# Chunk and weight loads issued further ahead, x laid out by chunks, two weight tiles converted among the first chunks

## The chip, the cores and the metric

The kernel runs on one core of one Trainium2 chip. The metric is the device time of one execution in microseconds. Three runs of the kernel before gave 604.84, 605.93 and 606.35 us; their median is 605.93 us.

## The reference

Three stages in a row, all in float32. First a gated linear attention with a state of 48 x 48 per head (batch 4, heads 8, 768 tokens, head size 48):

```python
f = 1.0 / (1.0 + np.exp(-f_logit))
for t in range(S):
    state = f[:, :, t, :, None] * state + np.einsum('bhd,bhe->bhde', k[:, :, t], v[:, :, t])
    y[:, :, t] = np.einsum('bhd,bhde->bhe', q[:, :, t], state)
```

Its result is put together to x of 3072 tokens x 384. Second a two-layer network with 2048 hidden units and a squared ReLU:

```python
h = np.maximum(x @ w_in, 0.0)
x = h * h @ w_out
```

Third a soft mixture of eight experts with four slots each: logits `x @ phi`, a softmax over the tokens that makes 32 slot inputs, two expert layers on those 32 rows, and a softmax over the slots that spreads their results back to the tokens.

## The kernel before

**Attention by chunks.** The 3072 tokens are cut into 24 chunks of 128 (six to each batch entry). A chunk needs one load of f, k and q together (`fkq`, 672 KB) into one of three slots g0 to g2 (`slot`, `SLOTS = 3`), and one of v (192 KB, `chunk_load`, lines 129 to 139) into one of three buffers. `prep(i)` (lines 144 to 182) makes running products of the gates and scales k and q with them: exponentials and logarithms on ScalarE (L156, L158, L169, L170), scans (L162) and products (L171, L177, L178, L179) on VectorE. Its last product, L179, is the last reader of the slot. `chunk(i)` (lines 270 to 281) has TensorE's part in five steps: transposes and their copy (L193, L195), scores (L205, L208), the state (L220, L228), values (L243, L250) and the result y (L254, L259). At its end SP issues six DMAs that put y into x, transposed and by rows: two of 72 KB (L265), two of 16 KB and two of 8 KB (L268).

**The two-layer network.** Four chunks make a block of 512 tokens, so x has six blocks (b) of [128, 3, 512], the 384 features in three groups of 128 (kt). The hidden units are cut into 16 tiles of 128 (ff). A step is one pair (b, ff): `layer1` and `layer2`. To keep float32 precision, x and the weights are each split into a high and a low part (`hl`: a cast on ScalarE, L113, and a difference on VectorE, L114), and every product becomes three matmuls of 512 columns (`mm3`, lines 118 to 120): nine for layer 1 (ph) and nine for layer 2 (o). 92 of the 96 steps go this way. The first four steps, block 0 with tiles 0 to 3, use unsplit float32 weights instead (`layer1_whole` L353, L384), whose matmuls take longer but need only the converted tile.

**Weights.** A tile's input and output weights come as 64-bit floats in one load of 768 KB (`w_load`, L305, `raw<-w`). `w_split` (lines 308 to 340) converts it to float32 in integer arithmetic: L315 and L319 on ScalarE, L320 and L321 on VectorE, and a last sum that makes the tile whole (L331 for tiles 0 to 3, L333 for the others). `w_parts` splits it. `WAHEAD = 4` says how many tiles are asked for ahead of the one that is converted. Raw, whole and split tiles share 16 buffers.

**Order.** `fast` and `fast_blocks` (lines 675 to 822) write the work down in one order. First chunks 0 to 2 and tiles 0 and 1 are loaded. `stream` then walks through the chunks: chunk i's five steps, with the preparation of a later chunk between them, and the load of a later one: chunk 3 after the last step of chunk 0, chunk 4 after that of chunk 1 (tiles 2 and 3 with them), and from chunk 3 on the load of chunk i + 2 behind the second step of chunk i. `upto(n)` advances the stream to its n-th step. After 23 steps (chunk 4, third step) tile 0 is converted and the steps of the network begin; step n = 0, 1, 2 each convert one more tile, from step 4 on each step converts the tile of its number, and each asks for tiles up to WAHEAD further on. The order of the steps is block 0 with tiles 0 to 3, block 1 with tiles 0 to 8, block 0 with the rest, block 1 with the rest (`TURNS`), and then block by block; the remaining chunks are worked in between (`target`).

This written order isn't the order on the engines. A planner takes it as a priority, estimates when each operand is ready, and gives every engine a fixed sequence from that: an instruction whose operands it believes to be there is put ahead of earlier written ones that still wait. For instance chunk 3's load stands on SP ahead of chunk 0's result, which is written first. At run time each engine works through its sequence strictly in order and waits where something is late. All DMAs here are issued by SP.

**The tail.** After the last block come the expert layers (`tail`, lines 575 to 672) and the output.

Of the kernel before, what the change touches and what calls it, by code (L numbers as in the profile page):

```python
# [18 lines left out]
HR = 64  # L19
# [15 lines left out]
LEAD = 4  # L35
SLOTS = 3
RAW = 5
WAHEAD = 4
AHEAD = 5
FIRST = 23  # L40
WARM = (3, 1, 3, 3)
# [1 line left out]

TURNS = ((0, 0, 4), (1, 0, 9), (0, 4, NFF), (1, 9, NFF))
ONACT = range(2, 8)
WHOLE = TURNS[0][2]
ORDER = (1, 0) + tuple(range(2, NB))
SECOND = 46
# [9 lines left out]
class K:  # L58
# [70 lines left out]
    def chunk_load(self, i):  # L129
        nc, ap = self.nc, self.ap  # L130
        fkq = self.slot(i % SLOTS)[:DD].rearrange("d (x p t) -> d x p t", x=3, p=NP)
        if i == 0:
            nc.sync.dma_start(out=fkq[:, 0], in_=self.A["fkq"][i][:, 0])
            nc.sync.dma_start(out=fkq[:, 1:], in_=self.A["fkq"][i][:, 1:])
        else:
            nc.sync.dma_start(out=fkq, in_=self.A["fkq"][i])
        v = ap.tile([128, DM], F32, tag="v", name="v", bufs=3)
        nc.sync.dma_start(out=v, in_=self.A["v"][i])
        return fkq[:, 0], fkq[:, 1], fkq[:, 2], v

# [91 lines left out]
    def values(self, i):  # L232
# [26 lines left out]
                nc.vector.tensor_tensor(y[:, :, r], y[:, :, r], py[j], ALU.subtract)  # L259
        if c == 0:  # L260
            self.x_alloc(b)
        xl = self.x[b][1].bitcast(F32)
        ts = slice(c * C, (c + 1) * C)
        for h in range(2):
            nc.sync.dma_start(out=xl[h * D : h * D + D, :, ts], in_=y[h * HR : h * HR + D, :KT])  # L265
        for h in range(2):
            for e, n, kt, o in PLACE[6 + h]:
                nc.sync.dma_start(out=xl[o : o + n, kt, ts], in_=y[h * HR + e : h * HR + e + n, KT])  # L268

    def chunk(self, i):  # L270

# [10 lines left out]


    def x_alloc(self, b):
        x = self.x_room(b % 2).rearrange("p (x k t) -> p x k t", x=2, k=KT)
        self.x[b] = x[:, 0], x[:, 1]

    def x_room(self, j):
        return self.fp.tile([128, 2 * KT * TB], F32R, tag=f"x{j}", name="x", bufs=1)

    def x_split(self, b, kt):
        xh, xl = self.x[b]
        self.hl(xh[:, kt], xl[:, kt], xl[:, kt].bitcast(F32))

    def w_load(self, ff):

# [50 lines left out]
    def layer1_whole(self, b, ff):  # L347

        nc, fp = self.nc, self.fp
        x, w = self.x[b][1].bitcast(F32), self.whole[ff]  # L350
        o = self.ps.tile([128, 512], F32, tag="h", name="ph", bufs=2)[:, :TB]
        for kt in range(KT):
            nc.tensor.matmul(out=o, lhsT=w[:, kt * 128 : kt * 128 + 128], rhs=x[:, kt], start=kt == 0, stop=kt == KT - 1)  # L353
        r = fp.tile([128, TB], F32, tag="r", name="r", bufs=1)
        nc.scalar.activation(r, o, AF.Relu)
        g = fp.tile([128, TB], F32, tag="gl", name="g2", bufs=2)
        nc.scalar.activation(g, r, AF.Square)
        return g, None

    def layer1(self, b, ff):  # L360
        nc, fp = self.nc, self.fp
        x, w = self.x[b], self.w[ff]
        ph = self.ps.tile([128, 512], F32, tag="h", name="ph", bufs=2)
        o = ph[:, :TB]
        for kt in range(KT):
            ks = slice(kt * 128, kt * 128 + 128)
            self.mm3(o, w[:, 0, ks], w[:, 1, ks], x[0][:, kt], x[1][:, kt], kt == 0, kt == KT - 1)
        r = fp.tile([128, TB], F32, tag="r", name="r", bufs=1)
        nc.scalar.activation(r, o, AF.Relu)  # L369
        gh = fp.tile([128, TB], F32R, tag="gh", name="gh", bufs=2)  # L370
        nc.scalar.activation(gh, r, AF.Square)  # L371
        nc.scalar.activation(r, r, AF.Square)  # L372
        gl = fp.tile([128, TB], F32R, tag="gl", name="gl", bufs=2)
        nc.vector.tensor_tensor(gl, r, gh.bitcast(F32), ALU.subtract)  # L374
        return gh, gl
# [320 lines left out]
    def fast_blocks(self, main, pst, ast, wst, raw):  # L696

        def stream():
            for i in range(2):
                yield from self.prep(i)  # L700
            for i in range(NCH):
# [3 lines left out]
                for j, n in enumerate((1, 1, 0, 0, 2) if ahead == 2 else (1, 1, 1, 0, 2)):  # L705
                    next(ch)
                    for _ in range(n):
                        next(pr, None)
                    new = i + 3 if i < 2 else i + 2
                    if j == (4 if i < 2 else 1) and i != 2 and new < NCH:  # L710
                        self.loaded[new] = self.chunk_load(new)
                        if new < 5:
                            more_w()
                    yield

# [2 lines left out]
                raw[len(raw)] = self.w_load(len(raw))  # L718

        st = stream()  # L720
        for _ in range(8):
            next(st)
        done = 0
        end = NCH * STEPS

# [22 lines left out]

        def split(b):
            if b in unsplit:  # L750
                for kt in range(KT):
                    self.x_split(b, kt)
                unsplit.remove(b)

        def begin1(b, ff):
# [6 lines left out]
        def part(ff):  # L762
            if ff in self.whole and ff not in self.w:
                self.w_parts(ff, self.whole[ff])

        upto(FIRST)
        unsplit = list(ORDER)
        self.w_split(0, raw[0], True)
        wn = 1
        posts = iter(())  # L770
        pend = begin1(0, 0)
        wait = 0
        for n, (b, ff) in enumerate(steps):
            if n == 3:
                self.consts3()
            if wn < WHOLE or WHOLE <= n and wn < NFF:
                while len(raw) < min(NFF, wn + WAHEAD):
                    more_w()
                self.w_split(wn, raw[wn], wn < WHOLE)
# [59 lines left out]
    def slow(self):  # L839
# [3 lines left out]
        with ExitStack() as main:  # L843
# [13 lines left out]
            with ExitStack() as st:  # L857
                self.pp = self.pool(st, "pp2")
                for b in range(NB):
                    self.x_alloc(b)  # L860
                    xh, xl = self.x[b]
                    self.hl(xh, xl, xT[:, :, b * TB : (b + 1) * TB])
                    for ff in range(NFF):
                        self.layer2(b, ff, self.layer1(b, ff), ff == 0, ff == NFF - 1)
                    for _ in self.post(b):
# [120 lines left out]
```

## Time and profile before

| what | value |
|---|---|
| median of three runs | 605.93 us |
| the profiled execution | 606.27 us |
| its span, first to last instruction | 604.5 us |
| TensorE (PE) busy | 574.9 us, 95% |
| TensorE weight loads (PEld) busy | 442.4 us, 73% |
| VectorE (DVE) busy | 328.7 us, 54% |
| ScalarE (ACT) busy | 314.8 us, 52% |
| DMA: time of packets on the data queue, share of 16 engines | 35.8% |
| moved | 69.59 MB |

The 1.77 us between the execution and its span lie ahead of the first and behind the last instruction. The busy time of TensorE is modelled at the ends of matmuls, which overlap, so a full TensorE is seen in the step from one matmul to the next (0.23 us for 512 columns at full clock) more than in the share. The kernel falls into stages: the first chunks with a start of the network (to some 87 us), the network with the remaining chunks (to some 545 us) and the tail.

### The profile page before, as it was taken

What the parts mean: (1) busy time and instruction counts of PE and PEld (TensorE: products, weight loads), DVE (VectorE), ACT (ScalarE), POOL (GpSimd) and SP (SyncE); (2) the same over time, 40 slices, a digit from 0 to 9 for tenths busy, and PEclk for the clock granted to TensorE, in tenths of its full rate; (3) what the DMA queues carried; (4) which work ended last, traced back from release to release, by engine and by line L of the source; (5) the groups of instructions that cost most, each with busy time, mean ns of one, the idle gap of its engine ahead of it and who ended that gap; (6) DMA issues with size and microseconds to landing.
All of it is one profiled execution on the core that took longest, in us unless ns stands there. A gap on an engine that the chain in (4) does not pass through costs nothing.

```text
span 604.5 us, 13326 instructions
## 1 busy us (share of the span) xinstructions
PE 574.9 (95%) x5587; PEld 442.4 (73%) x5587; DVE 328.7 (54%) x688; ACT 314.8 (52%) x577; POOL 4.0 (1%) x10
## 2 busy tenths in 40 slices
PE   4899899999999999999999999999999999998993
PEld 3784467788787878778877777887788887886372
DVE  6978989999825547454464552543332322213322
ACT  5647759996635546354455354544334544442122
POOL 0000000000000000000000000000000100000000
PEclk9999979999999999999999999999999999999898
DMA  9557558421321202202211210220000745554757
GB/s 290 181 154 236 160 190 287 151 67 47 105 60 40 73 2 73 59 16 73 73 46 28 74 63 18 79 79 3 15 14 12 263 135 177 168 199 157 262 205 272
DMA packets 28324, 69.59 MB, mean 115 GB/s; under 512 B 4464, under 2 KB 17008, under 8 KB 28256
## 3 DMA queue, kind: packets, MB, share of 16 engines
q1 hardware_dynamic: 28256, 68.65, 35.8%
q8 instruction: 46, 0.75, 0.5%
q14 instruction: 22, 0.18, 0.1%
HBM read 59.20 MB, written 4.72 MB: 106 GB/s over the span
## 4 chain that ended last, share of the span: by engine, by line
PE 77%; DVE 7%; DMA 6%; ACT 6%; issue 2%; SPq 1%; ACTq 0%; DVEq 0%
PE o L118 10%; PE ph L118 9%; PE o L120 9%; PE ph L120 9%; PE ph L119 9%; PE o L119 9%; DMA g<-fkq 4%; PE psm L243 3%; DMA raw<-w 2%; DVE ip L162 2%; PE hp L591 2%; PE psm L220 2%; PE psm L205 2%; PE so L615 2%; PE o L384 1%
## 5 line engine op out<-in xcount | busy, mean ns | idle before, releaser
L374 DVE TENSOR_TENSOR gl<-r,gh 128x512 fp32r<-128x512 f32 x92 | 63.5, 690 | 119.2 <-ACT r L372 118.6
L369 ACT ACTIVATE r<-ph 128x512 f32<-128x512 f32 x92 | 54.7, 595 | 119.9 <-PE ph L120 114.9
L118 PE MATMUL o<-gh,w 128*128 128x512 f32 x276 | 112.8, 409 | 0.0
L118 PE MATMUL ph<-x,w 128*128 128x512 f32 x276 | 111.5, 404 | 0.0
L119 PE MATMUL o<-gh,w 128*128 128x512 f32 x276 | 108.0, 391 | 0.0
L120 PE MATMUL o<-gl,w 128*128 128x512 f32 x276 | 106.3, 395 | 1.8 <-DVE gl L374 1.7
L120 PE MATMUL ph<-x,w 128*128 128x512 f32 x276 | 107.8, 391 | 0.0
L119 PE MATMUL ph<-x,w 128*128 128x512 f32 x276 | 107.6, 390 | 0.0
L120 PEld LDWEIGHTS o<-gl,w 128*128 128x128 f32 x276 | 51.6, 188 | 15.7 <-DVE gl L374 4.8
L118 PEld LDWEIGHTS ph<-x,w 128*128 128x128 f32 x276 | 51.8, 188 | 14.7 <-issue 4.1
L118 PEld LDWEIGHTS o<-gh,w 128*128 128x128 f32 x276 | 51.7, 187 | 12.6 <-ACT gh L371 0.5
L120 PEld LDWEIGHTS ph<-x,w 128*128 128x128 f32 x276 | 51.8, 188 | 11.5
L371 ACT ACTIVATE gh<-r 128x512 fp32r<-128x512 f32 x92 | 58.3, 634 | 2.0
L119 PEld LDWEIGHTS ph<-x,w 128*128 128x128 f32 x276 | 51.9, 188 | 9.7
L372 ACT ACTIVATE r<-r 128x512 f32<-128x512 f32 x92 | 58.0, 630 | 1.8
L119 PEld LDWEIGHTS o<-gh,w 128*128 128x128 f32 x276 | 51.9, 188 | 9.4
L156 ACT ACTIVATE g<-g 112x512 f32<-112x512 f32 (+1 forms) x25 | 15.1, 609 | 41.8 <-DMA g<-fkq 41.8
L243 PEld LDWEIGHTS psm<-q,S 48*48 48x48 f32 (+1 forms) x704 | 27.2, 147 | 9.7 <-issue 4.6
L243 PE MATMUL psm<-q,S 48*48 48x64 f32 (+1 forms) x704 | 31.5, 244 | 2.5 <-DVE S L226 1.3
L162 DVE TENSOR_TENSOR_SCAN ip<-g,ip,big 112x128 f32<-112x128 f32 x80 | 33.4, 467 | 0.4 <-ACT g L158 0.2
L220 PEld LDWEIGHTS psm<-v,n 64*48 64x48 f32 (+1 forms) x704 | 21.3, 146 | 10.8 <-issue 5.3
L169 ACT ACTIVATE g<-ip 112x512 f32<-112x512 f32 (+1 forms) x25 | 15.3, 611 | 26.2 <-DVE ip L162 26.1
(143 smaller groups left out, 683.0 us busy)
## 6 DMA issues: line engine op xcount, KB each, us to landing
m<-m SPq DMA_DIRECT2D x26, 768.0 KB, 4.4
g<-fkq SPq DMA_DIRECT2D x23, 672.0 KB, 5.2
raw<-w SPq DMA_DIRECT2D x16, 768.0 KB, 7.1
v<-v SPq DMA_DIRECT2D x24, 192.0 KB, 3.6
g<-m SPq DMA_DIRECT2D x6, 768.0 KB, 4.5
out_dram<-ob SPq DMA_DIRECT2D x18, 256.0 KB, 3.3
x<-y SPq DMA_DIRECT2D x48, 72.0 KB, 2.8
x<-y SPq DMA_DIRECT2D x48, 16.0 KB, 1.8
```

Source lines behind the costliest of these rows:

```text
L118: mm(out=out, lhsT=sh, rhs=mh, start=start, stop=False)
L119: mm(out=out, lhsT=sl, rhs=mh, start=False, stop=False)
L120: mm(out=out, lhsT=sh, rhs=ml, start=False, stop=stop)
L156: nc.scalar.activation(f[:, s], f[:, s], AF.Exp, scale=-1.0)
L162: nc.vector.tensor_tensor_scan(ip[:, p], f[:, p], big, 1.0 if first else self.ip[:, p, C - 1 : C], ALU.mult, ALU.min)
L169: nc.scalar.activation(f[:, s], ip[:, s], AF.Ln)
L220: nc.tensor.matmul(out=pu[c][m, p], lhsT=U["n"][r, p, m], rhs=U["v"][r, hd * D : hd * D + D], start=True, stop=True)
L243: nc.tensor.matmul(out=pz[h * HR : h * HR + m, p, r], lhsT=U["S"][c][d, p * D : p * D + m], rhs=U["q"][d, p, r], start=True, stop=True)
L369: nc.scalar.activation(r, o, AF.Relu)
L371: nc.scalar.activation(gh, r, AF.Square)
L372: nc.scalar.activation(r, r, AF.Square)
L374: nc.vector.tensor_tensor(gl, r, gh.bitcast(F32), ALU.subtract)
```

## The change

- `WAHEAD` goes from 4 to 6, and v has four buffers instead of three.
- The load of chunk 3 and of tiles 2 and 3 is asked for right after the first eight steps of the stream, which are the preparations of chunks 0 and 1.
- The load of chunk i + 3 (not i + 2) is asked for behind the second step of chunk i, for i from 1 to 20, and one more weight tile with it if fewer than WAHEAD are loaded ahead.
- Tile 0 is converted after 8 steps of chunks (third step of chunk 1) and tile 1 after 18 (third step of chunk 3), instead of at 23 and in step 0. Tiles 2 and 3 are converted in steps 0 and 1 instead of 1 and 2.
- x is laid out as [chunk, kt, 128 tokens] instead of [kt, 512 tokens]. A chunk's larger result DMA then writes 1536 bytes in a row in each partition instead of three times 512; a matmul of layer 1 reads its 512 columns as four runs of 128; the split of x goes by chunks (four operations of 384 columns on each engine) instead of by kt (three of 512).

```diff
-WAHEAD = 4
+WAHEAD = 6
+FIRSTW = 8, 18
...
-        v = ap.tile([128, DM], F32, tag="v", name="v", bufs=3)
+        v = ap.tile([128, DM], F32, tag="v", name="v", bufs=4)
...
-        xl = self.x[b][1].bitcast(F32)
-        ts = slice(c * C, (c + 1) * C)
+        xl = self.x[b][1].bitcast(F32)[:, c]
         for h in range(2):
-            nc.sync.dma_start(out=xl[h * D : h * D + D, :, ts], in_=y[h * HR : h * HR + D, :KT])
+            nc.sync.dma_start(out=xl[h * D : h * D + D], in_=y[h * HR : h * HR + D, :KT])
...
-        x = self.x_room(b % 2).rearrange("p (x k t) -> p x k t", x=2, k=KT)
+        x = self.x_room(b % 2).rearrange("p (x c k t) -> p x c k t", x=2, c=NC, k=KT)
...
-    def x_split(self, b, kt):
+    def x_split(self, b, c):
         xh, xl = self.x[b]
-        self.hl(xh[:, kt], xl[:, kt], xl[:, kt].bitcast(F32))
+        self.hl(xh[:, c], xl[:, c], xl[:, c].bitcast(F32))
...
-            self.mm3(o, w[:, 0, ks], w[:, 1, ks], x[0][:, kt], x[1][:, kt], kt == 0, kt == KT - 1)
+            self.mm3(o, w[:, 0, ks], w[:, 1, ks], x[0][:, :, kt], x[1][:, :, kt], kt == 0, kt == KT - 1)
...
-                    new = i + 3 if i < 2 else i + 2
-                    if j == (4 if i < 2 else 1) and i != 2 and new < NCH:
-                        self.loaded[new] = self.chunk_load(new)
-                        if new < 5:
+                    if j == 1 and 0 < i < NCH - SLOTS:
+                        self.loaded[i + SLOTS] = self.chunk_load(i + SLOTS)
+                        if len(raw) < wn + WAHEAD:
                             more_w()
...
         st = stream()
+        wn = 0
         for _ in range(8):
             next(st)
+        self.loaded[SLOTS] = self.chunk_load(SLOTS)
+        for _ in range(2):
+            more_w()
...
+        for n in FIRSTW:
+            upto(n)
+            self.w_split(wn, raw[wn], True)
+            wn += 1
         upto(FIRST)
         unsplit = list(ORDER)
-        self.w_split(0, raw[0], True)
-        wn = 1
...
-            if wn < WHOLE or WHOLE <= n and wn < NFF:
+            if wn < min(WHOLE, n + 3) or WHOLE <= n and wn < NFF:
```

What is left out takes the same layout of x through `layer1_whole`, the copy out of layer 1 and a second path of the kernel that these inputs don't take.

## Rows read from the trace of the kernel before

**Rows 1.** The page's first part: busy us (share of the span) and instructions.

```profile
PE 574.9 (95%) x5587; PEld 442.4 (73%) x5587; DVE 328.7 (54%) x688; ACT 314.8 (52%) x577; POOL 4.0 (1%) x10
```

**Rows 2.** Windows by stage: PE, PEld, DVE, ACT, POOL busy, PEclk, DMA share, GB/s.

```profile
0.00:15.00 15.00, 6.12 (x117) 5.39 (x118) 9.36 (x27) 7.46 (x15) 1.10 (x8) 1.00 0.91 288
...
8.00:45.00 37.00, 32.15 (x634) 29.01 (x637) 31.12 (x70) 20.07 (x37) 0.00 (x0) 1.00 0.68 205
45.00:87.00 42.00, 38.71 (x451) 22.01 (x443) 36.41 (x72) 29.17 (x53) 0.00 (x0) 0.92 0.62 182
87.00:150.00 63.00, 62.82 (x485) 49.53 (x484) 62.32 (x104) 54.02 (x96) 0.00 (x0) 1.00 0.45 151
150.00:190.00 40.00, 38.42 (x282) 30.10 (x280) 21.18 (x45) 21.91 (x40) 0.00 (x0) 1.00 0.27 71
190.00:545.00 355.00, 354.36 (x3136) 282.01 (x3137) 155.28 (x332) 172.31 (x318) 2.85 (x2) 1.00 0.25 75
```

**Rows 3.** The chain of waits, 20 to 100 us: start, us, what.

```profile
30.69 7.15 DMA raw<-w
...
64.78 7.78 DMA raw<-w
```

**Rows 4.** Timeline of ScalarE: start, us, instruction, [idle before <- what ended it].

```profile
18.56 0.91 ACT L315 ACTIVATE raw<-raw 128x768 int32<-128x768 uint32 x1
...
27.65 0.91 ACT L315 ACTIVATE raw<-raw 128x768 int32<-128x768 uint32 x1 [1.42 <-DMA raw<-w]
29.90 0.63 ACT L156 ACTIVATE g<-g 112x512 f32<-112x512 f32 x1 [1.33 <-DMA g<-fkq]
...
37.86 0.93 ACT L315 ACTIVATE raw<-raw 128x768 int32<-128x768 uint32 x1 [2.35 <-DMA raw<-w]
...
42.68 0.63 ACT L156 ACTIVATE g<-g 112x512 f32<-112x512 f32 x1 [1.78 <-DMA g<-fkq]
...
72.59 0.97 ACT L315 ACTIVATE raw<-raw 128x768 int32<-128x768 uint32 x1 [1.40 <-DMA raw<-w]
```

**Rows 5.** Waits of TensorE, 0 to 87 us: total us, times, longest.

```profile
PE psm L220 <- ACT n L195: 2.1, 1, 2.1
...
PE ph L353 <- DVE wn L331: 0.9, 1, 0.9
```

**Rows 6.** Windows of 3 us around the late stall, columns as in rows 2.

```profile
72.00:75.00 3.00, 0.93 (x36) 0.65 (x33) 3.00 (x7) 2.41 (x5) 0.00 (x0) 1.00 0.30 57
75.00:78.00 3.00, 2.96 (x24) 1.37 (x26) 1.97 (x5) 1.75 (x3) 0.00 (x0) 0.58 1.04 302
78.00:81.00 3.00, 3.00 (x80) 2.94 (x77) 2.14 (x4) 0.66 (x2) 0.00 (x0) 0.50 0.68 257
81.00:84.00 3.00, 3.00 (x9) 1.44 (x7) 2.51 (x5) 2.35 (x5) 0.00 (x0) 0.78 0.13 29
```

**Rows 7.** Timeline of SP's DMA issues, 0 to 60 us.

```profile
8.90 0.33 SPq L136 DMA_DIRECT2D g<-fkq  x1
...
22.64 0.53 SPq L138 DMA_DIRECT2D v<-v  x1
...
36.57 0.58 SPq L136 DMA_DIRECT2D g<-fkq  x1
```

**Rows 8.** The differences of line 114 by shape: ns min/median/max, first and last start.

```profile
L114 DVE TENSOR_TENSOR x<-x x18: 682/685/693, 74.2 to 471.6; 128x512 fp32r<-128x512 f32 x18
L114 DVE TENSOR_TENSOR w<-whi,w x12: 930/950/959, 81.8 to 144.5; 128x768 fp32r<-128x768 f32 x12
```

**Rows 9.** Timelines of SP and VectorE around a late chunk load.

```profile
155.36 20.23 SPq L136 DMA_DIRECT2D g<-fkq  x2
...
174.51 0.69 DVE L179 TENSOR_TENSOR q<-g,t 112x512 f32<-112x512 f32 x1 [2.52 <-PE psm L243]
```

**Rows 10.** The chain of waits: a wide matmul and a group of short ones.

```profile
161.36 0.23 PE o L118
...
249.07 1.01 PE psm L243 x29
```

More of the change, by code (lines that the diff above doesn't have):

```diff
@@ L261, in values @@
             self.x_alloc(b)
-        xl = self.x[b][1].bitcast(F32)
-        ts = slice(c * C, (c + 1) * C)
+        xl = self.x[b][1].bitcast(F32)[:, c]
         for h in range(2):
-            nc.sync.dma_start(out=xl[h * D : h * D + D, :, ts], in_=y[h * HR : h * HR + D, :KT])
+            nc.sync.dma_start(out=xl[h * D : h * D + D], in_=y[h * HR : h * HR + D, :KT])
         for h in range(2):
             for e, n, kt, o in PLACE[6 + h]:
-                nc.sync.dma_start(out=xl[o : o + n, kt, ts], in_=y[h * HR + e : h * HR + e + n, KT])
+                nc.sync.dma_start(out=xl[o : o + n, kt], in_=y[h * HR + e : h * HR + e + n, KT])
     def chunk(self, i):
@@ L352, in layer1_whole @@
         for kt in range(KT):
-            nc.tensor.matmul(out=o, lhsT=w[:, kt * 128 : kt * 128 + 128], rhs=x[:, kt], start=kt == 0, stop=kt == KT - 1)
+            nc.tensor.matmul(out=o.rearrange("p (c t) -> p c t", c=NC), lhsT=w[:, kt * 128 : kt * 128 + 128], rhs=x[:, :, kt], start=kt == 0, stop=kt == KT - 1)
         r = fp.tile([128, TB], F32, tag="r", name="r", bufs=1)
@@ L363, in layer1 @@
         ph = self.ps.tile([128, 512], F32, tag="h", name="ph", bufs=2)
-        o = ph[:, :TB]
+        o = ph[:, :TB].rearrange("p (c t) -> p c t", c=NC)
         for kt in range(KT):
             ks = slice(kt * 128, kt * 128 + 128)
-            self.mm3(o, w[:, 0, ks], w[:, 1, ks], x[0][:, kt], x[1][:, kt], kt == 0, kt == KT - 1)
+            self.mm3(o, w[:, 0, ks], w[:, 1, ks], x[0][:, :, kt], x[1][:, :, kt], kt == 0, kt == KT - 1)
         r = fp.tile([128, TB], F32, tag="r", name="r", bufs=1)
-        nc.scalar.activation(r, o, AF.Relu)
+        nc.scalar.activation(r, ph[:, :TB], AF.Relu)
         gh = fp.tile([128, TB], F32R, tag="gh", name="gh", bufs=2)
@@ L750, in split @@
             if b in unsplit:
-                for kt in range(KT):
-                    self.x_split(b, kt)
+                for c in range(NC):
+                    self.x_split(b, c)
                 unsplit.remove(b)
@@ L861, in slow @@
                     xh, xl = self.x[b]
-                    self.hl(xh, xl, xT[:, :, b * TB : (b + 1) * TB])
+                    self.hl(xh, xl, xT[:, :, b * TB : (b + 1) * TB].rearrange("p k (c t) -> p c k t", c=NC))
                     for ff in range(NFF):
```

## The prediction

> **What bounds the kernel now.** First the page's busy shares: TensorE counts as busy for 95% of the span [rows 1], so the question is where it isn't, or where it runs slowly. Second the busy time by stage [rows 2]. From 87 us to 545 us TensorE is full but for 0.18 us in 87 to 150, 1.58 us in 150 to 190 and 0.64 us after; that work is the same before and after. What can move the end is the stage ahead of it: from 8 to 87 us TensorE lacks 4.85 + 3.29 us, VectorE 5.88 + 5.59 us. Third, the chain of waits between 20 and 100 us: its two longest pieces are loads of weight tiles, 7.15 us from 30.69 and 7.78 us from 64.78 [rows 3]. Such a piece is not all loss: while a load is under way the engines do other work, and only the end of it holds someone. Who is held is read from ScalarE's timeline [rows 4]: converts (L315) wait 1.42, 2.35 and 1.40 us for a weight tile, and exponentials (L156) 1.33 and 1.78 us for a chunk. ScalarE runs its queue in order, so what stands behind a waiting convert waits too. At 72.59 that is, two operations on, the copy L195, for which TensorE waits 2.1 us [rows 5].
>
> That late stall costs twice. By windows of 3 us [rows 6], TensorE is busy for 0.93 us in 72 to 75, and then the granted clock falls to 0.58, 0.50 and 0.78 of full speed in the next three: the lower of its two levels (1.2 of 2.4 GHz) for (1 - 0.58) / 0.5 x 3 = 2.5, then 3.0 and 1.3 us, together 6.8 us.
>
> **The change part by part,** against the profiled execution: 606.27 us, its span 604.5; the median of the runs is 605.93, 0.34 below.
>
> *Weight loads earlier.* Tiles 2 and 3 are issued behind the results of chunks 0 and 1 now, tile 2 right after the value load v of chunk 3 at 22.64, which waits for one of three v buffers [rows 7], tile 3 at 30.69 [rows 3]. With the fourth v buffer, and both tiles asked for right after chunk 3, they can follow that chunk's load at 8.90 [rows 7]. Tiles 4 to 7 each move from a step of the network (tile 6: 64.78 [rows 3]) to chunks 1 to 4, tile 6 by some 25 us, and SP has no more to issue than before. So the waits of L315 should go. The late one: 2.1 us of TensorE, **-2.1**. With it the fall of the clock: half of 6.8 us is 3.4 us, but VectorE works for 6.62 of the 9 us [rows 6], so no more than 2.4 comes out before it is late next: **-2.4** (ends 0, if TensorE goes idle elsewhere, and -3.4, if VectorE's work there can come earlier).
>
> *Chunk loads earlier.* Chunk 5's load is issued at 36.57 [rows 7], behind chunk 2's result; its slot, chunk 2's, is free from that chunk's preparation on, well before its result. Asked for a chunk earlier it stands behind chunk 1's result, at about 30 us, and the waits of 1.33 and 1.78 us go. Together with the early converts ScalarE waits 1.42 + 1.33 + 2.35 + 1.78 = 6.88 us [rows 4]. That can't all be gained: TensorE lacks 4.85 us in 8 to 45, VectorE 5.88, and part of both is the recurrence from chunk to chunk. Ends 0 and -4.9; I take the middle, **-2.5**.
>
> *Two tiles converted among the first chunks.* The products L331 of tiles 0 and 1 (0.95 us of VectorE each, L331 ends when the tile is whole) come some steps earlier, and tiles 2 and 3 one step earlier each. TensorE waits for such a tile once, 0.9 us [rows 5]. Price: two products more in a stretch in which VectorE has 5.88 us free. I take **-0.5** (ends +1.0 and -0.9).
>
> *x by chunks.* A split is four pairs of operations of 384 columns in place of three of 512. VectorE takes 685 ns for 512 columns and 950 for 768 [rows 8], so 555 for 384: 4 x 555 - 3 x 685 = +0.17 us a block. Four of six blocks are split where VectorE is half idle [rows 2]; blocks 0 and 1 lie in the full stretch: **+0.3**. ScalarE's part is as small and has room there. The result's larger DMA writes runs of 1536 bytes instead of 512, the four small ones stay, and SP issues as many as before: nothing, since the last small one ends the group. The matmuls read x in four runs of 128 columns: no row shows that, and I cost it at nothing (ends 0 and a rival below).
>
> *Late holes.* The 1.58 us in 150 to 190 belong to chunk loads that wait for a slot: SP stands 20.23 us in two issues from 155.36, until VectorE's L179 at 174.51 has read the slot [rows 9]. Slots stay three, so asking earlier doesn't help: nothing (ends -1.6 and +1.0, the same hole again).
>
> *Handed back.* What comes earlier than 87 us meets a stretch where VectorE has 0.68 of 63 us free. From 8 to 150 it has 12.15 us free in all, of which the 7.5 would take more than half; I charge **+1.0** (ends 0 and +4).
>
> Sum: -2.1 - 2.4 - 2.5 - 0.5 + 0.3 + 1.0 = -6.2, so 600.1 in the profiled execution and **599.7** as a median.
>
> **The rivals.**
> *ScalarE held at the start (slower).* The planner puts converts well ahead of the code's place (tile 6's convert belongs to step 6, and it runs before step 4 begins). If it puts tile 2's where tile 1's is now, at 18.56 us [rows 4], it waits for a queue that is already full: the loads issued up to 10 us would be four chunks of 672 + 192 KB, four tiles of 768 KB and 96 KB of constants, 6.8 MB, at the 288 GB/s of the first 15 us [rows 2] landed 23.5 us after 1.5, at 25 us. ScalarE would stand 6.4 us in front of the chunks, and the early gain of 2.5 would go: 599.7 + 2.5 + 6.4 = 608.6. It decides from a stand of 3.7 us on. For it: three such waits in the trace now. Against: even crowded, the tiles land before the 27.65 and 37.86 at which they are converted now [rows 4]. The Trainium skill's DMA: Bandwidth & Descriptors (Queues, rings and completion order) says that each DMA engine consumes the descriptors of one issuer's row in ring order; by that a chunk's load behind two weight tiles would wait for both. In rows that is the same stand with an exponential in the convert's place: two tiles of 768 KB at 288 GB/s are 5.5 us, and 599.7 + 2.5 + 5.5 = 607.7; its chance is part of this rival's. No row here tells ring order from mere crowding.
>
> *x's runs cost TensorE (slower).* 828 matmuls of layer 1 would restart at three breaks each. The nearest row is the short matmuls L243: 1.01 us for 29 of 64 columns, 35 ns each, against 0.23 us / 512 x 64 = 29 ns of a wide one [rows 10], so at most 6 ns a break: 828 x 3 x 6 ns = +14.9, 614.6. It turns the sign from 2.5 ns on. Against it: the wide matmul's columns lie next to each other in runs of 512 bytes. The Trainium skill's SBUF — State Buffer (Door 1, the note on cachelines) puts the penalty of a stride at crossings of 16-byte lines, of which the breaks add none; no run here shows it yet.
>
> *VectorE gives half back.* The moved products and exponentials only queue on VectorE before 150 us: half of 6.2, so 603.
>
> *Everything goes.* Late 2.1 + 3.4, early 4.9, the tile 0.9, the holes 1.6, nothing handed back: -12.9 + 0.3, so 605.93 - 12.6 = 593.3.
>
> *The loads don't really move.* The planner or a full queue leaves weights and chunks where they land now: 605.5 to 606.5.
>
> **How the numbers follow.** Forecast 0.42 (597.5 to 602), everything 0.17, half back 0.15, no change 0.10, ScalarE held 0.12, x's runs 0.04. A run of this kernel can be told from no change by about 0.3%, 1.8 us. Faster: 0.42 + 0.17 + 0.13 of half back = 0.72; same 0.02 + 0.10 = 0.12; slower 0.16. The range 594 to 608 leaves out x's runs, half of ScalarE held and the lower half of everything, about 0.18.
>
> **What would show it.** Right: tiles 2 and 3 issued near 10 us, tile 6 before 45; no wait of L315 over 1 us; granted clock 1.00 from 60 to 90; the first split matmul (L118, now where the stage from 87 us begins) some 6 us earlier, and the distance from there to the end unchanged. Wrong: L315 waiting at 16 to 25 us; a new stretch of half clock; a wide matmul's step above 0.23 us in layer 1 and not in layer 2; VectorE full before 87 with TensorE waiting for it; holes after 150 that grow by what the start gained.

## The result, and the profile after

The changed kernel takes 609.42 us (median of four runs, 609.33 to 609.94); the kernel before, on the same chip, 605.38 us (604.49 to 606.35). The ratio is 1.0068, 95% interval [1.0049, 1.0087]: slower by 0.7%, and 1.4 us above the end of the forecast range. The profiled execution has a span of 607.6 us against 604.5.

The first split matmul of the network, the milestone that the forecast named, starts at 92.67 us. Before, it started at 86.9: it is 5.8 us later, not 6 earlier. From there to the end 514.9 us pass instead of 517.6. 5.8 - 2.7 = 3.1 us is the whole difference of the spans.

In the kernel after, a line up to the result's DMAs has a number one higher than before: L157 is L156 of the kernel before. The windows by stage, columns as in [rows 2]:

```profile
8.00:45.00 37.00, 28.49 (x583) 25.85 (x585) 31.39 (x70) 21.86 (x40) 0.00 (x0) 1.00 0.95 288
45.00:87.00 42.00, 39.28 (x476) 24.11 (x472) 37.16 (x74) 28.96 (x53) 0.00 (x0) 1.00 0.55 164
87.00:150.00 63.00, 59.90 (x420) 46.69 (x419) 60.61 (x103) 49.93 (x88) 0.00 (x0) 0.97 0.37 119
150.00:190.00 40.00, 39.83 (x346) 31.99 (x346) 20.92 (x44) 22.53 (x39) 0.00 (x0) 1.00 0.23 65
190.00:545.00 355.00, 354.42 (x3137) 281.81 (x3136) 156.68 (x337) 174.51 (x324) 2.85 (x2) 1.00 0.24 73
```

Against [rows 2]: the clock of 45 to 87 us is back at 1.00, but TensorE lacks 8.51 us in 8 to 45 (4.85 before), and a new hole of 3.10 us stands in 87 to 150 (0.18 before). The holes of 150 to 190 shrank from 1.58 to 0.17.

What the forecast said of the loads came. SP's issues in the kernel after: tiles 2 and 3 together near 10 us, tile 6 at 41 us.

```profile
10.40 0.96 SPq L305 DMA_DIRECT2D raw<-w  x2
...
41.36 0.43 SPq L305 DMA_DIRECT2D raw<-w  x1
```

And ScalarE's waits from 0 to 125 us (total, times, longest) for a chunk and for a tile; before, the same two lines of this view had 6.7 us in 5 waits and 5.2 us in 3, the long ones of which are in [rows 4]:

```profile
ACT g L157 <- DMA g<-fkq: 3.9, 2, 2.4
...
ACT raw L315 <- DMA raw<-w: 0.7, 1, 0.7
```

So data came earlier, and the network's full stage began later. Where is seen in the timeline of ScalarE after (start, length, instruction, [idle before <- what ended it]):

```profile
30.97 0.60 ACT L255 ACTIVATE y<-psm 112x512 f32<-112x512 f32 x1 [2.92 <-PE psm L244]
...
33.61 0.91 ACT L319 ACTIVATE whi<-raw 128x768 f32<-128x768 f32 x1 [0.34 <-DVE wn L331]
...
34.51 0.62 ACT L157 ACTIVATE g<-g 112x512 f32<-112x512 f32 x1
...
35.70 0.91 ACT L315 ACTIVATE raw<-raw 128x768 int32<-128x768 uint32 x1
38.53 0.63 ACT L170 ACTIVATE g<-ip 112x512 f32<-112x512 f32 x1 [1.92 <-DVE ip L163]
...
39.73 0.58 ACT L255 ACTIVATE y<-psm 112x512 f32<-112x512 f32 x1
...
46.35 0.63 ACT L170 ACTIVATE g<-ip 112x512 f32<-112x512 f32 x1 [3.22 <-DVE ip L163]
...
48.18 0.59 ACT L255 ACTIVATE y<-psm 112x512 f32<-112x512 f32 x1
...
92.11 0.51 ACT L114 CAST x<-x 128x384 fp32r<-128x384 f32 x1 [2.92 <-issue]
```

and in that of VectorE:

```profile
30.49 0.56 DVE L320 TENSOR_SCALAR whi<-whi 128x768 int32<-128x768 int32 x1
31.08 0.96 DVE L321 SCALAR_TENSOR_TENSOR whi<-raw,whi 128x768 int32<-128x768 int32 x1
...
32.62 0.95 DVE L331 CUSTOM_DVE_ANT_0 wn<-raw,whi 128x1536 uint16<-128x1536 uint16 x1
...
35.01 0.55 DVE L320 TENSOR_SCALAR whi<-whi 128x768 int32<-128x768 int32 x1
...
35.97 0.95 DVE L321 SCALAR_TENSOR_TENSOR whi<-raw,whi 128x768 int32<-128x768 int32 x1
36.83 1.60 DVE L163 TENSOR_TENSOR_SCAN ip<-g,ip,big 112x128 f32<-112x128 f32 x4
```

From 30.49 to 36.92 us VectorE does 0.56 + 0.96 + 0.95 + 0.55 + 0.95 = 3.97 us of weight conversion, and only then chunk 4's scan L163. On ScalarE chunk 4's exponential (L157) stands behind L319 of these conversions and starts at 34.51; before, it started at 29.90 [rows 4]. Its logarithm L170 then waits 1.92 us for the scan, and the copy of chunk 3's result (L255, 39.73) stands behind that. In the timeline of ScalarE before, the same two pairs of logarithm and copy are

```profile
34.22 0.63 ACT L169 ACTIVATE g<-ip 112x512 f32<-112x512 f32 x1 [0.97 <-DVE ip L162]
...
38.69 0.57 ACT L254 ACTIVATE y<-psm 112x512 f32<-112x512 f32 x1
...
44.80 0.60 ACT L254 ACTIVATE y<-psm 112x512 f32<-112x512 f32 x1 [1.49 <-PE psm L243]
...
47.66 0.63 ACT L169 ACTIVATE g<-ip 112x512 f32<-112x512 f32 x1 [1.23 <-DVE ip L162]
```

Chunk 4's logarithm stood ahead of chunk 3's copy before as well, but it ran at 34.22. For the next pair the order itself has turned: chunk 5's logarithm (46.35) now stands ahead of the copy of chunk 4's result (48.18), where before it stood behind it (47.66 against 44.80). So conversions of weights that come early hold a chunk's preparation, and an instruction for a later chunk holds the result of an earlier one. That the planner put them there because it believed their data to be there follows from how it works; its estimates aren't in the trace.

On TensorE the order has changed on a larger scale. Its timeline after, at the start of the network and at the first split matmul:

```profile
56.15 6.83 PE L353 MATMUL ph<-x,wn 128*128 128x512 f32 x12
...
91.03 0.66 PE L221 MATMUL psm<-v,n 64*64 64x48 f32 x16 [1.86 <-DVE a L209]
92.67 0.50 PE L119 MATMUL ph<-x,w 128*128 128x512 f32 x1 [0.98 <-ACT x L114]
```

Chunk 5 as a whole now stands ahead of the network's first matmul, which starts at 56.15 instead of 45.55. In exchange the unsplit steps run closer together and end at 87.5, only 1.3 us later than before (86.2); but chunks 6 and 7 stand behind them, and chunk 7's y copy runs at 83.7 instead of 80.3 us. The first split step needs block 1, and chunk 7 is its last. Its x is cast at 92.11 us, and for that TensorE stands still.

Of the 5.8 us by which the first split matmul is late, 3.4 are chunk 7's copy. The other 2.4 lie between copy and matmul, and the layout has a part in them: with x by kt, the first cast of a block needs three of a chunk's six result DMAs, and with x by chunks it needs all six. SP's last issues of chunk 7's result after, with the cast at 92.11 above:

```profile
86.70 2.49 SPq L268 DMA_DIRECT2D x<-y  x4
```

and before, with ScalarE's first cast:

```profile
83.30 2.50 SPq L268 DMA_DIRECT2D x<-y  x4
...
85.89 0.62 ACT L113 CAST x<-x 128x512 fp32r<-128x512 f32 x1
```

The cast starts 2.9 us after the end of the last issue, where before it started 0.1 us after it. What this costs in the end is not seen in a ratio (no_layout below). Windows of 3 us there:

```profile
87.00:90.00 3.00, 2.17 (x54) 1.48 (x52) 3.00 (x7) 2.06 (x4) 0.00 (x0) 1.00 0.21 51
90.00:93.00 3.00, 0.99 (x17) 0.84 (x18) 3.00 (x5) 0.90 (x2) 0.00 (x0) 1.00 0.34 64
93.00:96.00 3.00, 3.00 (x9) 2.31 (x8) 2.82 (x6) 1.99 (x4) 0.00 (x0) 0.53 0.98 377
96.00:99.00 3.00, 3.00 (x13) 2.20 (x11) 3.00 (x6) 1.92 (x4) 0.00 (x0) 0.90 1.01 422
```

TensorE is idle for 0.83 + 2.01 = 2.8 us, and the granted clock then falls to 0.53 and 0.90: (0.47 + 0.10) / 0.5 x 3 = 3.4 us at the lower level. The late stall of [rows 6] is gone from its place, and another, for chunk 7's x, stands some 18 us later. VectorE has work for the full 3.00 us of the two windows from 87 to 93.

One thing can be closed here. The chain of waits after, a matmul of layer 2 (o) and one of layer 1 (ph, which reads the new layout):

```profile
161.36 0.23 PE o L121
...
162.98 0.23 PE ph L119
```

The step is 0.23 us in both, as in [rows 10]. From 190 to 545 us the median step from one matmul of ph to the next is 227 ns before and after: four runs of 128 columns cost nothing that is seen.

### The profile page after: what moved, and what is told of

The parts are those of the page before. It is cut to its first block, busy times and chain, and to the rows that moved or that the text cites. A ratio compares the mean times of both kernels' runs of the same rounds, so it can differ in the third digit from the quotient of the medians.

```text
span 607.6 us, 13356 instructions
## 1 busy us (share of the span) xinstructions
PE 573.4 (94%) x5587; PEld 443.8 (73%) x5587; DVE 329.9 (54%) x694; ACT 317.1 (52%) x583; POOL 4.0 (1%) x10
## 4 chain that ended last, share of the span: by engine, by line
PE 76%; ACT 7%; DMA 6%; DVE 5%; SPq 3%; issue 2%; DVEq 0%; ACTq 0%
PE o L119 10%; PE ph L119 9%; PE o L121 9%; PE ph L120 9%; PE ph L121 9%; PE o L120 9%; PE psm L244 3%; DMA x<-y 2%; DMA g<-fkq 2%; PE hp L591 2%; PE psm L206 2%; PE so L615 2%; PE psm L221 2%; PE psm L251 2%; PE psm L415 1%
## 5 line engine op out<-in xcount | busy, mean ns | idle before, releaser
L369 ACT ACTIVATE r<-ph 128x512 f32<-128x512 f32 x92 | 54.6, 594 | 117.8 <-PE ph L121 112.0
L121 PEld LDWEIGHTS o<-gl,w 128*128 128x128 f32 x276 | 51.6, 188 | 13.7 <-DVE gl L374 2.8
L163 DVE TENSOR_TENSOR_SCAN ip<-g,ip,big 112x128 f32<-112x128 f32 x80 | 33.5, 467 | 2.6 <-ACT g L159 2.5
L157 ACT ACTIVATE g<-g 112x512 f32<-112x512 f32 (+1 forms) x25 | 15.2, 612 | 37.1 <-DMA g<-fkq 37.1
L170 ACT ACTIVATE g<-ip 112x512 f32<-112x512 f32 (+1 forms) x25 | 15.3, 612 | 31.6 <-DVE ip L163 30.8
```

The costliest lines, as they stand in the source:

```text
L121: mm(out=out, lhsT=sh, rhs=ml, start=False, stop=stop)
L157: nc.scalar.activation(f[:, s], f[:, s], AF.Exp, scale=-1.0)
L163: nc.vector.tensor_tensor_scan(ip[:, p], f[:, p], big, 1.0 if first else self.ip[:, p, C - 1 : C], ALU.mult, ALU.min)
L170: nc.scalar.activation(f[:, s], ip[:, s], AF.Ln)
L369: nc.scalar.activation(r, ph[:, :TB], AF.Relu)
```

## The experiments

The theory after this reading: **order**. The change moves arrivals, the planner makes another fixed order from its estimate of them, and that order delays the chunks' results; at first it was put more narrowly, that chunk 5 passes the network's first matmul. The rivals: **crowding** (earlier loads delay other transfers), and **one bad part** (one of the four parts costs, the others gain). Ratios are to the kernel before, run beside each kernel on the same chip, with 95% intervals.

### One part taken out, one part alone

Four kernels leave one part out of the change. no_layout takes back all lines of the diff on x:

```diff
-        xl = self.x[b][1].bitcast(F32)[:, c]
+        xl = self.x[b][1].bitcast(F32)
+        ts = slice(c * C, (c + 1) * C)
```

> The changed kernel with x in its old layout (and split by kt). Layout theory (four runs cost TensorE, or the casts by chunk crowd ScalarE): back to 605 or less. Order theory (chunk loads asked for a chunk earlier let chunk 5 pass the network's first matmul on TensorE, which then starts at 56 us instead of 45.5) and crowding theory (weights ahead delay chunk loads and results): stays at 608 to 611, first L353 still near 56 us.

no_chunks loads the chunks as before, into three v buffers, with the weights early:

```diff
-        v = ap.tile([128, DM], F32, tag="v", name="v", bufs=4)
+        v = ap.tile([128, DM], F32, tag="v", name="v", bufs=3)
...
+                    new = i + 3 if i < 2 else i + 2
+                    if j == (4 if i < 2 else 1) and i != 2 and new < NCH:
+                        self.loaded[new] = self.chunk_load(new)
                     if j == 1 and 0 < i < NCH - SLOTS:
-                        self.loaded[i + SLOTS] = self.chunk_load(i + SLOTS)
...
-        self.loaded[SLOTS] = self.chunk_load(SLOTS)
```

> The changed kernel with chunk loads and v buffers as before; weights, conversions and layout as changed. Order theory: the first L353 stands behind chunk 4 again, starts before 48 us, and the time falls to 601 to 605. Crowding theory: weights still stand ahead in the queue, 607 to 610. Conversion theory (VectorE's converts in front of the chunk chain): 607 to 610.

no_weights asks for weights as before, no more than four tiles ahead:

```diff
-WAHEAD = 6
+WAHEAD = 4
...
-                        if len(raw) < wn + WAHEAD:
+                        if i == 1:
                             more_w()
...
-        for _ in range(2):
-            more_w()
+        more_w()
```

> The changed kernel with weight loads as before (four ahead, two with chunks 3 and 4); chunk loads, conversions and layout as changed. Crowding theory: 604 to 606. Order theory: the first L353 stands inside chunk 5, so part of the loss stays, 607 to 610, and the waits of L315 come back.

no_convert converts the tiles where they were converted before:

```diff
-        for n in FIRSTW:
-            upto(n)
-            self.w_split(wn, raw[wn], True)
-            wn += 1
         upto(FIRST)
...
+        self.w_split(0, raw[0], True)
+        wn = 1
...
-            if wn < min(WHOLE, n + 3) or WHOLE <= n and wn < NFF:
+            if wn < WHOLE or WHOLE <= n and wn < NFF:
```

> The changed kernel with tiles 0 to 3 converted as before (from step 0 on). Conversion theory: 604 to 606. Order theory: the first L353 still stands behind chunk 5's state, 608 to 612, since the tiles are late besides. Crowding theory: 608 to 611.

Three kernels put one part into the kernel before: chunks_alone the loads of chunks with v's fourth buffer (tiles 2 and 3 are asked for with chunks 3 and 4, as before),

```diff
+        self.loaded[SLOTS] = self.chunk_load(SLOTS)
+        more_w()
...
+                    if j == 1 and 0 < i < NCH - SLOTS:
+                        self.loaded[i + SLOTS] = self.chunk_load(i + SLOTS)
```

> The kernel before with the chunk loads alone a chunk earlier and four v buffers. Order theory (chunk 5, loaded earlier, passes the network's first matmul on TensorE): first L353 after 49 us, chunk 6 late, time up by 1 to 5 us over the kernel before. Weight theory (only the early weight loads cost, through what they put ahead on SP and the engines): the same as before or faster by 1 to 3 us.

weights_alone the earlier requests for weights,

```diff
-WAHEAD = 4
+WAHEAD = 6
...
+                    if j == 1 and 0 < i < NCH - SLOTS:
+                        if len(raw) < wn + WAHEAD:
                             more_w()
...
+        for _ in range(2):
+            more_w()
```

> The kernel before with the weight loads alone earlier (two after chunk 1's preparation, one with each chunk, six ahead). Weight theory: slower by 4 us or more, since chunk 3's load, which the kernel before issues at 8.9 us, now stands behind two weight tiles and chunk 0's result on SP, near 22 us. Order theory: first L353 stays behind chunk 4, so the same as before or faster.

and convert_alone the conversions, the reverse of no_convert's diff.

> The kernel before with tiles 0 to 3 converted earlier and nothing else. Without it the changed kernel was slower, so it should help by itself: 1 to 3 us faster than before, the wait of the first network matmuls for a tile gone. Conversion theory (VectorE's converts hold the chunks): 1 to 3 us slower.

Measured, with times read from each profile (us): start of the network's first matmul (L353), chunk 7's y copy, end of the unsplit steps, first split matmul; one profile each, which can stand some 2 us beside the kernel's median (598.45 against 600.81 us for early_chunks, 603.29 against 601.23 for early_loads, 614.19 against 612.01 for no_convert, 608.77 against 606.11 for chunks_alone). The kernels ran on several chips, on which the kernel before has medians from 602.75 to 605.38 us, so small differences between rows say little. The last five rows belong to the next two parts.

| kernel | ratio [95%] | first L353 | chunk 7's y | unsplit ends | first split |
|---|---|---|---|---|---|
| before | 1 | 45.5 | 80.3 | 86.2 | 86.9 |
| after | 1.0068 [1.0049, 1.0087] | 56.1 | 83.7 | 87.5 | 92.7 |
| no_layout | 1.0077 [1.0049, 1.0106] | 55.7 | 83.2 | 87.1 | 90.4 |
| no_chunks | 1.0130 [1.0096, 1.0164] | 51.6 | 83.2 | 86.2 | 93.0 |
| no_weights | 1.0034 [1.0011, 1.0057] | 49.9 | 79.0 | 83.9 | 88.0 |
| no_convert | 1.0132 [1.0098, 1.0166] | 55.3 | 83.9 | 88.8 | 94.1 |
| chunks_alone | 1.0051 [1.0028, 1.0073] | 50.6 | 81.5 | 89.7 | 91.2 |
| weights_alone | 1.0134 [1.0096, 1.0172] | 50.1 | 84.8 | 89.7 | 90.5 |
| convert_alone | 1.0123 [1.0085, 1.0160] | 46.4 | 82.5 | 87.5 | 90.9 |
| early_loads | 0.9945 [0.9927, 0.9964] | 45.6 | 77.3 | 82.2 | 84.2 |
| early_chunks | 0.9940 [0.9918, 0.9961] | 44.0 | 75.7 | 80.6 | 82.1 |
| early_weights | 1.0144 [1.0118, 1.0170] | 51.3 | 81.3 | 86.2 | 91.1 |
| x_order | 1.0191 [1.0160, 1.0222] | 55.0 | 87.1 | 92.1 | 95.8 |
| convert_order | 1.0032 [1.0010, 1.0054] | 46.2 | 76.5 | 81.4 | 84.9 |

What follows. The layout neither costs nor gains anything that can be measured in the end (1.0077 without it, 1.0068 with it). "One bad part" falls: each of the other three slows the kernel when it is alone. Of the three taken out of the change only the weights may give something back (1.0068 to 1.0034, with intervals that overlap); taking out the chunks' loads or the conversions makes it worse. Parts that add up to less than each costs alone are not costs of operations. And convert_alone speaks for order by itself: it adds no operation, moves the conversions of tiles 0 and 1 among the chunks and those of tiles 2 and 3 by a step, asks for later tiles a step earlier at most, and costs 1.2%.

Three expectations missed. By the order theory as it was first put, no_chunks was to fall to 601 to 605 us and weights_alone to be no slower than before; convert_alone was to move by 1 to 3 us, one way or the other. They take 1.0130, 1.0134 and 1.0123. In convert_alone the network's first matmul starts at 46.4, 0.9 us later than before, and the kernel is slower all the same: the place of that one matmul is not what costs. A kernel with the network's first step written after 18 steps of the chunks, which was to try that place by itself, has no measured time.

### The loads alone, with the order held

To part order from crowding, the planner's freedom was taken away. In the next three kernels every instruction of TensorE, ScalarE and VectorE is tied behind the one that precedes it in the sequence of the kernel before (`PLACES` lists that sequence as numbers, 3736, 554 and 683 of them). Only SP's sequence, and with it the times of arrival, differ from before.

```diff
+        order = np.frombuffer(zlib.decompress(base64.b85decode(table)), np.int16)[:upto]
+        for a, b in zip(order, order[1:]):
+            tc.add_manual_dep(mine[b], mine[a].name, mybir.DependencyInfo(mybir.DependencyClass.NoSync, mybir.DependencyReason.DATA), reason="pin")
...
         k.fast()
+        pin(tc)
```

`mine` is an engine's instructions as they are written, `order` their places in the held sequence. early_loads has the change's chunk and weight loads, early_chunks those of chunks_alone, early_weights those of weights_alone, all three the old layout and conversions. In their traces the recorded instructions of ScalarE and VectorE, 577 and 688, stand in the sequence of before. The kernel before with its own sequence tied wasn't run; that the ties themselves change nothing is assumed.

> The change's loads (chunks three ahead, weights six tiles ahead) with the instruction order of TensorE, ScalarE and VectorE pinned, instruction by instruction, to that of the kernel before; old layout of x, no tile converted among the first chunks. Only SP's stream and so the times of arrival differ from before. Theory (the planner's order delays the chunks): TensorE's idle time from 9 to 45 us falls back to about the 4.3 us of before, the first y copies stand within 1 us of before's, ScalarE's waits for fkq and raw shrink as they did after, and the gain that was forecast for the loads comes out: ratio 0.990 to 1.000. Rival (the earlier transfers themselves delay the chunks' loads and results): order changes nothing, idle from 9 to 45 us stays at 8 us or more, ratio 1.005 to 1.013 as in the kernels with both loads.

> Only the chunks' loads earlier (with v's fourth buffer), the order of the three engines pinned to before's. With the planner's own order this edit made 1.0051. Theory: with the order held it is no slower than before, 0.993 to 1.001. Rival (transfers): 1.003 to 1.007, as with the planner's order.

> Only the weights' loads earlier, the order of the three engines pinned to before's. With the planner's own order this edit made 1.0134. On SP chunk 3's load now stands behind four weight tiles and chunk 0's result, so it is issued near 22 us where before had it at 8.9. Theory with that in it: ScalarE's exponential of chunk 3 (in the pinned order near 28 us) waits some 2 us longer than before, the rest is as before: 0.997 to 1.006, well under 1.013. Rival (transfers crowd everything): 1.010 to 1.015.

The same loads that made 1.0132 in the planner's order (no_convert, which also has the layout that costs nothing) make 0.9945 in the order of before; the chunks' loads went from 1.0051 to 0.9940. The order alone is worth (1.0132 - 0.9945) x 605 = 11 us. SP isn't held in either, but its first 59 issues, up to 58 us, have the same sequence in both. Crowding as the rival had it, 1.005 to 1.013 in any order, is out for these loads. Windows of early_loads, columns as in [rows 2]:

```profile
45.00:87.00 42.00, 37.41 (x494) 21.56 (x490) 39.26 (x76) 30.35 (x55) 0.00 (x0) 1.00 0.73 218
87.00:150.00 63.00, 62.81 (x475) 49.80 (x474) 61.87 (x107) 54.97 (x96) 0.00 (x0) 1.00 0.30 100
```

The clock is 1.00 in 45 to 87 us, and no hole follows. TensorE's timeline of early_loads at the end of the unsplit steps:

```profile
74.78 1.12 PE L384 MATMUL o<-g,wn 128*128 128x512 f32 x2
...
77.68 4.56 PE L384 MATMUL o<-g,wn 128*128 128x512 f32 x10
```

and of the kernel before, where the stall and the half clock of [rows 6] stand there:

```profile
75.71 2.07 PE L384 MATMUL o<-g,wn 128*128 128x512 f32 x2
...
81.09 5.14 PE L384 MATMUL o<-g,wn 128*128 128x512 f32 x10
```

The same two matmuls took 2.07 us before and take 1.12 now, the same ten 5.14 and 4.56. That is the gain which the forecast had in mind. Details of the expectation missed: TensorE's idle time from 9 to 45 us was to fall back to the 4.3 us of before, and it is 7.3, hardly less than the 8.1 of the kernel after; and the copies of chunks 1 to 3 stand 1.4 to 1.7 us behind before's, not within 1 us. So idle time in that window doesn't tell a good order from a bad one. Chunk 7's result does so here (77.3 against 83.7 us), but not in every row of the table: in no_weights and convert_order it is earlier than before (79.0 and 76.5 against 80.3), and both are slower.

early_weights missed as well: 0.997 to 1.006 was expected, and it takes 1.0144, as much as with the planner's order. Not crowding in general, though, since early_loads has the same weight loads. One load on SP stands out. The timeline of SP in early_weights:

```profile
22.39 0.58 SPq L136 DMA_DIRECT2D g<-fkq  x1
```

and of its ScalarE:

```profile
27.34 0.63 ACT L156 ACTIVATE g<-g 112x512 f32<-112x512 f32 x1 [5.31 <-DMA g<-fkq]
```

With four tiles asked for first, chunk 3's load stands behind chunk 0's result and is issued at 22.39 us instead of 8.90 [rows 7]; ScalarE waits 5.31 us for it. Chunk 1's result is issued at 31.58 us instead of 26.15 and chunk 3's at 45.51 instead of 40.11; of this 1.0 us is left at chunk 7's copy, and the first split matmul is 4.2 us late. SP's sequence is a part of the order, and it was not held here. How much of early_weights' 1.0144 or of weights_alone's 1.0134 is this one load wasn't tried apart, but weights_alone and no_chunks issue it at about 22.5 us too.

### The order for early conversions

Is the order bad only because loads are where they were? x_order is the whole change, with the three engines' sequence tied to the one that the planner makes when conversions and layout are changed and the loads are not. Against the kernel after, with a table of that sequence in `PLACES`:

```diff
         k.fast()
+        pin(tc)
```

> The whole change (early loads, x by chunks, two tiles converted among the first chunks), with TensorE's, ScalarE's and VectorE's order pinned to the one that the planner makes for the same kernel with the loads where they were before, that is with two conversions moved but without the estimate that chunks and weights are there earlier. Theory (order decides, and the order for early conversions is a worse one by itself: alone it cost 1.0123): the loads give back what they gave in a held order (0.994) and the conversions' order keeps its cost, less what of it was waiting for late tiles: 0.998 to 1.008, above the 0.9945 of the order of before. Rival (the conversions' order is only bad while the tiles come late; with tiles there at 14 to 18 us it is as good as the old one): 0.990 to 0.996.

1.0191, slower than theory and rival had it, and for a reason of its own. SP's timeline in x_order shows chunk 3's result:

```profile
42.77 1.51 SPq L265 DMA_DIRECT2D x<-y  x2
44.97 5.83 SPq L268 DMA_DIRECT2D x<-y  x4
```

ScalarE, which casts that x for the network:

```profile
55.51 0.51 ACT L114 CAST x<-x 128x384 fp32r<-128x384 f32 x1 [6.47 <-DMA x<-y]
```

and TensorE's waits from 45 to 87 us:

```profile
PE ph L353 <- DMA x<-y: 7.5, 1, 7.5
```

Two chunk loads and two tiles were issued between 38.88 and 42.3 us, just ahead of this result. Its four small DMAs take 5.83 us to issue, where they take 2.49 elsewhere in the same timeline, and x is there only at 55.5 us. Part of that is SP itself, as its waits from 40 to 56 us show:

```profile
SPq L268 <- DMA raw<-w: 3.6, 2, 2.6
```

Eight semaphores go round among the program's DMAs, and an issue waits until the one eight before it has landed: the first small one starts at 44.97 us, when the chunk load of 38.88 has landed (44.95), and two more wait for the two tiles. The other part is the transfer: the result lands at 54.6 to 55.2 us, just behind the chunk load of 41.13 (53.9). Crowding does exist, then, where large loads stand directly ahead of a result that TensorE needs next. The Trainium skill's DMA: Bandwidth & Descriptors (Queues, rings and completion order), by which each DMA engine takes one issuer's descriptors in ring order, agrees with it, but no run here tells ring order from shared bandwidth. So x_order doesn't answer its question. convert_order asks it again, without the early weights: it is early_chunks, with its chunk loads and the old layout, with the sequence of convert_alone in place of before's. Against early_chunks, beside the other table:

```diff
+        for n in FIRSTW:
+            upto(n)
+            self.w_split(wn, raw[wn], True)
+            wn += 1
         upto(FIRST)
...
-        self.w_split(0, raw[0], True)
-        wn = 1
```

> Only the chunks' loads earlier, old layout of x, with the three engines' order pinned to the one the planner made for the kernel with two conversions moved and the loads as before (that kernel took 1.0123). It is early_chunks (0.994) with another order and the same loads, and without the earlier weights that stood ahead of chunk 3's result in x_order. Theory (the conversions' order is the worse one by itself, since it puts chunk 6 behind two more steps of the network): chunk 7's y copy stands near 80 us, some 4 us behind early_chunks' 75.7, the first split matmul 8 to 9 us behind that copy; ratio 1.002 to 1.010. Rival (only late tiles or results made that order slow, as the wait for x in x_order): chunk 7's copy within 1.5 us of early_chunks', ratio 0.990 to 0.998.

1.0032 [1.0010, 1.0054] against 0.9940 [0.9918, 0.9961] for early_chunks: the same instructions with the same chunk loads, in another order (and with later tiles asked for a step earlier at most), cost 0.9%, some 5.5 us. SP was not held here either: its sequence differs from the 32nd issue on (chunk 6's load at 32.87 instead of 36.68 us), and its part isn't told from that of the other engines. The ratio is where the theory put it, but its details are not: chunk 7's copy stands at 76.5, only 0.8 us later than in early_chunks, the first split matmul 2.8 us later, and the rest of the difference comes after it (521.0 us to the end against 514.6, in single profiles). There the granted clock is 0.97 against 1.00 in 87 to 150 us, and TensorE's holes in 150 to 190 are 2.30 against 1.03 us; which instruction costs it stays open.

early_chunks and early_loads beat both kernels: 600.81 and 601.23 against the 604.45 us of before on their chip.

## Why the prediction was wrong

- *What bounds the kernel.* Right for the change itself in the main: the stage ahead of the first split matmul moved the end. But the distance from there to the end changed by 2.7 us, not by nothing, and in other orders by more (521.0 us in convert_order, 517.6 before): a new order reaches past 87 us.
- *Weight loads earlier, -2.1 and -2.4.* The rows came as said (L315 waits 0.7 us in all, clock 1.00 from 60 to 90). The gain didn't: a stall and a fall of the clock stand at 87 to 99 us instead, where chunk 7's x is late. With the order held the gain is there, but it is the chunk loads' with tiles 2 and 3 close behind them: the further weights add nothing to them (0.9945 against 0.9940).
- *Chunk loads earlier, -2.5 (ends 0 and -4.9).* With the order held, 0.6% or 3.6 us for these loads with all that follows from them. In the planner's order the same loads cost 0.5%.
- *Two tiles converted, -0.5 (ends +1.0 and -0.9).* Sign and size wrong. No operation was added, as said, but alone the edit costs 1.23% or 7.4 us, and the order made for it 0.9% with the chunks' loads early.
- *x by chunks, +0.3,* and the rival *x's runs cost TensorE*: the layout can't be told from nothing in the ratios, and the matmul step is 0.23 us in both layers. The sum's reason for the DMAs, that the last small one ends the group, doesn't hold: the old layout's first cast needs only the first of the four small ones, the new one's needs the last. The Trainium skill's SBUF — State Buffer (Door 1, the note on cachelines) is borne out as far as this: breaks after 512 bytes cost nothing here.
- *Late holes, 0.* They shrank from 1.58 to 0.17 us, nearly the low end of that term. Why wasn't tried.
- *Handed back, +1.0 (ends 0 and +4).* It assumed that something had been gained by 87 us. VectorE is full from 87 to 93 us as this term and the rival *VectorE gives half back* had it, but early_loads has nearly as little room there (61.87 of 63 us busy in 87 to 150) and no hole: a full VectorE alone doesn't make it.

**The step that failed** is in the parts on loads and conversions: each was priced on the timeline of before, as if the engines would go through the same sequence with fewer waits. The sum holds no term for a new sequence, though the text that it rests on says that the planner makes the sequence from estimated arrivals, and though every edit here changes such an estimate. Held to the old sequence, the loads come out at 0.9945, 605.93 x 0.9945 = 602.6, about half of the -6.0 that the sum gave the loads less what is handed back. The planner's own sequence then turns that into the loss: 1.0132 for these loads without the conversions, 1.0068 for the whole change.

The rival *ScalarE held at the start* had the right sign and part of the mechanism, the planner putting converts forward. But it saw one convert that waits for its tile, and that wait is absent (0.7 us). What holds the chunks is work that hardly waits (0.34 us for L319 at 33.61) and stands ahead of theirs.

## What to carry to other kernels

Where a planner fixes each engine's order from estimated arrivals, an edit that moves a load is also an edit of the order: price both, and look in the new order for work of later stages ahead of results of earlier ones. To find out which of the two a result is due to, hold the old order and change the loads alone; if that is faster, the held order is the version to keep. No single milestone replaced the time of the whole kernel here: neither idle time summed over a window nor chunk 7's result nor the first split matmul puts the kernels of the table in the order of their ratios. And large loads issued directly ahead of a result on the same queue delayed it (x_order).

## What the runs showed of the hardware

**The granted clock of the first chunks can't be taken from the clock column of one profile.** The kernel before, from 27 to 33 us by windows (here the columns are PE busy, PEclk, DMA share, GB/s):

```profile
27.00:33.00 6.00, 5.57 (x98) 1.00 0.72 194
```

The same window of early_chunks:

```profile
27.00:33.00 6.00, 5.24 (x92) 0.50 0.81 234
```

A group of short matmuls in it, in TensorE's timeline of the kernel before:

```profile
30.61 1.13 PE L250 MATMUL psm<-a,v 64*48 64x64 f32 x30
```

and such groups in that of early_chunks, the second in a stretch with a clock of 1.00:

```profile
30.71 1.13 PE L250 MATMUL psm<-a,v 64*48 64x64 f32 x30
...
75.46 0.66 PE L250 MATMUL psm<-a,v 64*48 64x64 f32 x30
```

One prints a full clock from 27 to 33 us and the other half of it, and thirty equal matmuls take 1.13 us in both, against 0.66 at full clock. So both kernels seem to have been at the lower level there. The sum of the prediction doesn't use the clock of that stretch.

**The first loads land earlier or later from profile to profile.** Chunk 1's load is issued at 3.07 us (3.06 in early_loads) behind the same five DMAs in before, after, early_loads and early_chunks, and ScalarE gets it at 9.08, 10.41, 11.13 and 8.67 us. Up to 8.9 us SP's sequence is the same in all four. Whether that is chance isn't shown, but times read from one profile may differ by as much (2.5 us) for that alone; the ratios come from many runs.
